# First K and a third of the first Q by the plain queue, cast in parts; the mask row table as 24 rows twice onto zeros

## The chip, the cores and the metric

One core of one Trainium2 chip runs the kernel. The metric is the device time of one execution, in microseconds, of the slowest core (here the only one). Executions of this kernel scatter by about 1 us and now and then more, also from chip to chip, so each ratio below sets a kernel against the kernel before in rounds on the same chip.

## The reference, cut to what matters

```python
# attention: batch 4, heads 8, sequence 768, head_dim 64, blocks of 32 rows
scores = q @ k^T / 8            # (4, 8, 768, 768)
mask   = |block_i - block_j| <= 1 or first/last block or 3 sampled blocks per block row
attn   = softmax(where(mask, scores, -1e9))
x      = (attn @ v), heads side by side         # (3072, 512)
# gated FFN: d_model 512, d_ff 1536
out    = (sigmoid(x @ w_gate) * (x @ w_val)) @ w_out    # (3072, 512)
```

All inputs are float32, `sampled_blocks` int64. The kernel computes in float16 with float32 accumulation.

## The kernel before

The kernel is a list of operations, each with a rough duration and a priority. A planner in the kernel (`Plan.run`) plays them through with assumed durations and landing times. Its outcome is a **fixed order** of instructions for each engine. On the chip the engines took their instructions in that order and waited where an operand was not there yet (1.60 us on ScalarE in the kernel before). So an operation that the planner thought would be ready early, but is not, holds up all that stands behind it on its engine.

Attention is done in 12 chunks of 256 queries (3 per batch), each for 4 pairs of heads; one pair of a chunk takes 3 score tiles, so 3 exps on ScalarE. The first chunk (`n == 0`) adds the mask as a bias inside the score product, the others multiply by a 0/1 mask on VectorE. FFN work for finished chunks is mixed in.

```python
FIRST = [("q", 0), ("k", 1), ("q", 1), ("k", 2), ...]    # casting loads of batch 0, in this order
# ... cut ...
# planner: when a load that was issued at `now` is assumed to have landed
                if o.dma:
                    first = now + (3.2 if e == "POOL" else 1.9)
                    if o.dma > 0.15:
                        first = dma_free = max(dma_free, first) + o.dma
                    o.seen = first + 0.3 + o.slack
# ... cut ...
# head: identity, first K and mask row table on the plain queue (SP), two small block tables on ACT's
    P.op("SP", 0.4, ... nc.sync.dma_start(ident16(), id_h.ap()) ..., prio=-99)
    P.op("ACT", 0.4, ... nc.scalar.dma_start(sbi(), sampled_blocks) ..., prio=-90)
    P.op("ACT", 0.4, ... nc.scalar.dma_start(mi(), mi_h.ap()) ..., prio=-89)
    P.op("SP", 0.5, ... nc.sync.dma_start(e24(), e24_h.ap()) ..., prio=-94.5)   # 128 rows, mostly zeros
    load("k", 0, 0, -95)
    P.op("ACT", 0.83, lambda t=t, c=c: nc.scalar.copy(c(), t()), reads=[t], writes=[c], prio=-67)
    for i, (nm, p) in enumerate(FIRST):
        last_in = load_half(nm, 0, p, -60 + i, ...)           # GpSimd: float32 in HBM to float16
    for p in range(NP):
        turn_pe("k", 0, p, every, -40 + 2 * p)                # transposes on TensorE
        turn_pe("q", 0, p, early, -39.5 + 2 * p)
# ... cut: block tables -> bias rows (VectorE, TensorE) ...
# loads of the next batch, plain queue, behind the third of three output-weight loads
                for nm in "kqv":
                    o = load(nm, b + 1, p, seq + p, behind=turned[:-2][-2:],
                             **(dict(after=[w_out[8]], sync="o") if b == 0 else {}))
                    o.slack = 1.5
                for nm in "kq":
                    turned.append(turn_dma(nm, b + 1, p, seq + p + CAST_LATE * b))   # cast, then DMA transpose
                cast_v(b + 1, p, seq + p + CAST_LATE * b)
```

The softmax here doesn't subtract the row's maximum and nothing guards it: scores larger than these inputs give would overflow.

## Time and profile before

| what | where it is read | value |
|---|---|---|
| time, median of 4 runs | result | 297.81 us (297.67 to 298.46) |
| TensorE busy | page, part 1 | 289.7 of 295.6 us |
| first exp starts | timeline | 9.03 us |
| second FFN weight landed, first gate matmul | issues, timeline | 25.1, 25.35 us |
| next batch's first load issued | timeline | 40.24 us |
| TensorE idle from 45 to 50 us | windows | 0.75 us |

Lines of the page of the kernel before: busy time by engine (part 1), and the chain that ended last (part 4).

```profile
PE 289.7 (98%) x3417; PEld 211.3 (72%) x3417; DVE 192.4 (65%) x448; ACT 212.5 (72%) x329; POOL 13.4 (5%) x22
...
PE 82%; DMA 13%; POOL 2%; issue 1%; SPq 0%; ACT 0%; DVE 0%; POOLq 0%
```

TensorE looks full. But "busy" spans overlap (a gate matmul is 0.27 us long in the page, and the next starts 0.11 us after it), and 13% of the chain of waits is DMA, all of it before 50 us.

The timeline of the head. Columns: start, duration, engine, line and operation, output and input, count, and in brackets the idle time just before with what ended it.

```profile
1.38 0.31 ACTq L338 DMA_DIRECT2D mi<-bb_mdet_iota  x1
...
3.78 0.22 DVE L509 TENSOR_TENSOR eqs<-mi,sbi 24x72 f32<-24x72 f32 x1 [2.52 <-DMA mi<-bb_mdet_iota]
...
4.11 0.83 ACT L451 CAST k_first<-ks 128x768 f16<-128x768 f32 x1 [1.10 <-DMA ks<-in_k_dram]
...
6.26 0.35 PE L427 MATMUL psum<-ident,q 128*64 128x128 f16 x4
...
7.76 0.53 PE L427 MATMUL psum<-ident,k 128*64 128x128 f16 x12 [0.28 <-DMA k<-in_k_dram]
...
8.38 0.28 PE L582 MATMUL psum<-bias,e 64*128 64x256 f16 x2
...
9.03 1.94 ACT L598 ACTIVATE pt<-psum 128x1024 f16<-128x1024 f32 x2 [4.10 <-PE psum L582]
```

The block table is there at 3.78 us. The transposes of the *next* pair's K (7.76, waiting for their load) stand ahead of the first scores (8.38).

ScalarE from 15 to 30 us: the exps of the first chunk run into those of the second (12 of the first chunk, then on), with short waits.

```profile
14.64 2.98 ACT L598 ACTIVATE pt<-psum 128x1024 f16<-128x1024 f32 x3 [0.69 <-PE psum L582]
17.85 5.71 ACT L598 ACTIVATE pt<-psum 128x1024 f16<-128x1024 f32 x6 [0.24 <-PE psum L582]
23.95 3.77 ACT L598 ACTIVATE pt<-psum 128x1024 f16<-128x1024 f32 x4 [0.39 <-PE psum L582]
```

Windows: stretch and its length, then busy time of PE, PEld, DVE, ACT, POOL (with counts), the granted clock, DMA share and GB/s.

```profile
5.00:10.00 5.00, 4.72 (x72) 2.93 (x71) 2.57 (x6) 0.97 (x2) 4.29 (x7) 1.00 1.25 180
10.00:15.00 5.00, 4.81 (x90) 3.28 (x85) 3.48 (x8) 4.26 (x6) 2.91 (x4) 1.00 1.31 202
...
20.00:25.00 5.00, 4.72 (x95) 3.51 (x92) 4.12 (x11) 4.61 (x6) 0.00 (x0) 1.00 1.16 209
...
45.00:50.00 5.00, 4.25 (x68) 3.22 (x67) 2.10 (x7) 3.76 (x7) 0.00 (x0) 1.00 1.08 286
```

The DMA share, a sum of the packets' times, passes 1 here (1.31 from 10 to 15 us). In windows of 2 us it stays at 1.13 or more from 4 to 38 us; from 38 to 41 us it falls to between 0.53 and 0, since the next batch's loads are issued only at 40.24. The timeline behind the last of these rows:

```profile
45.69 0.83 ACT L402 CAST q<-qs 128x768 f16<-128x768 f32 x1 [1.60 <-DMA qs<-in_q_dram]
...
47.19 0.83 ACT L393 CAST v<-vs 128x768 f16<-128x768 f32 x1 [0.38 <-DMA vs<-in_v_dram]
...
48.67 0.42 DVE L632 TENSOR_TENSOR x<-psum,rz 128x256 f16<-128x256 f32 x1
...
49.15 0.28 PE L657 MATMUL psum<-ident,x 128*128 128x128 f16 x2 [0.74 <-DVE x L632]
```

ScalarE stands 1.60 us in front of a cast whose load (next batch's Q) has not landed. Gate functions stand behind it, VectorE behind them, TensorE last. The last wait in this chain is not that one but the next: the cast of V, whose load landed at 47.16. A gate function follows at 47.92, VectorE at 48.33 and 48.67, TensorE at 49.15.

### The profile page before, as it was taken

Reading aid. Unit: us, or ns where it says so; the run is one execution under the profiler, and the core shown is the slowest. Engines: PE = TensorE matmul, PEld = TensorE weight load, DVE = VectorE, ACT = ScalarE, POOL = GpSimd, SP = SyncE. Lnnn points to the kernel's source line nnn. Section 1 sums busy time; section 2 is a strip of 40 time slices with the busy share of each in tenths; the row PEclk is TensorE's granted clock in tenths of the full one; section 3 lists DMA queues with packets and bytes.
Section 4 is the critical chain, followed back from the end, with each engine's and each line's share of the span. In section 5 each row is a group of like instructions: output and inputs, shape, how many; then the busy total and the mean of one; then the engine's idle time right before and its main releaser. Section 6 shows DMA issues by size and latency. Waiting matters only on the chain.

```text
span 295.6 us, 8119 instructions
## 1 busy us (share of the span) xinstructions
PE 289.7 (98%) x3417; PEld 211.3 (72%) x3417; DVE 192.4 (65%) x448; ACT 212.5 (72%) x329; POOL 13.4 (5%) x22
## 2 busy tenths in 40 slices
PE   8999998999999999999999999999999999999995
PEld 7676875786587587578578678667767768778673
DVE  3659995799677677577767657657657656634230
ACT  2699987889888789797588578478478478434331
POOL 8630000000000000000000000000000000000000
PEclk9999999999999999999999999999999999999999
DMA  7999969999999969940210210210120120120102
GB/s 157 199 211 210 206 171 283 311 297 271 272 244 248 228 96 308 172 115 2 62 47 0 65 47 3 55 54 2 31 77 2 27 83 3 27 82 0 38 35 72
DMA packets 50316, 35.56 MB, mean 120 GB/s; under 512 B 31080, under 2 KB 47336, under 8 KB 50280
## 3 DMA queue, kind: packets, MB, share of 16 engines
q1 hardware_dynamic: 43520, 28.16, 38.5%
q0 software_dynamic: 6688, 6.88, 14.1%
q8 instruction: 26, 0.43, 0.6%
q14 instruction: 10, 0.08, 0.1%
q10 hardware_dynamic: 72, 0.01, 0.0%
HBM read 28.55 MB, written 6.29 MB: 118 GB/s over the span
## 4 chain that ended last, share of the span: by engine, by line
PE 82%; DMA 13%; POOL 2%; issue 1%; SPq 0%; ACT 0%; DVE 0%; POOLq 0%
PE psum L683 40%; PE psum L727 21%; PE psum L582 10%; PE psum L621 10%; DMA wo<-in_moe_w_out_dram 8%; DMA q<-in_q_dram 3%; DMA vs<-in_v_dram 2%; POOL q L409 1%; POOL k L409 1%; POOL wo L481 1%; SPq L371 0%; POOL vh L409 0%; PE psum L657 0%; DVE h L709 0%; ACT tg L702 0%
## 5 line engine op out<-in xcount | busy, mean ns | idle before, releaser
L598 ACT ACTIVATE pt<-psum 128x1024 f16<-128x1024 f32 x144 | 143.9, 1025 | 38.1 <-PE psum L582 37.9
L606 DVE TENSOR_TENSOR pt<-pt,mask 128x1024 f16<-128x1024 f16 x132 | 90.4, 689 | 44.1 <-ACT pt L598 43.7
L683 PE MATMUL psum<-x,wg 128*128 128x256 f16 x576 | 86.6, 273 | 0.2 <-DVE h L709 0.2
L683 PE MATMUL psum<-x,wv 128*128 128x256 f16 x576 | 86.7, 273 | 0.0
L709 DVE SCALAR_TENSOR_TENSOR h<-tg,psum 128x256 f16<-128x256 f32 x144 | 56.8, 416 | 21.3 <-ACT tg L702 21.2
L727 PE MATMUL psum<-wo,h 128*128 128x512 f16 (+1 forms) x300 | 66.8, 371 | 0.0
L702 ACT ACTIVATE tg<-psum 128x256 f32<-128x256 f32 x144 | 55.2, 388 | 14.1 <-PE psum L683 11.3
L683 PEld LDWEIGHTS <-wg 128*128 128x128 f16 x576 | 54.7, 98 | 11.5 <-issue 4.2
L683 PEld LDWEIGHTS <-wv 128*128 128x128 f16 x576 | 53.8, 98 | 11.9 <-issue 6.1
L727 PEld LDWEIGHTS <-h 128*128 128x128 f16 x300 | 27.5, 98 | 30.6 <-issue 4.0
L582 PE MATMUL psum<-qT,kT 64*128 64x256 f16 x576 | 48.5, 272 | 0.3 <-ACT pt L598 0.3
L621 PEld LDWEIGHTS <-pt 128*128 128x128 f16 x1152 | 40.4, 97 | 4.3 <-issue 1.3
L621 PE MATMUL psum<-v,pt 128*128 128x65 f16 x1152 | 42.2, 193 | 0.0
L582 PEld LDWEIGHTS <-kT 64*128 64x128 f16 x576 | 23.4, 94 | 14.5 <-issue 11.0
L744 ACT ACTIVATE y<-psum 128x512 f32<-128x512 f32 (+1 forms) x21 | 12.1, 577 | 21.9 <-PE psum L727 20.0
L632 DVE TENSOR_TENSOR x<-psum,rz 128x256 f16<-128x256 f32 x48 | 20.4, 424 | 1.6
L629 DVE RECIPROCAL rz<-psum 128x4 f32<-128x4 f32 x48 | 8.6, 179 | 15.6 <-PE psum L621 15.1
L356 PE MATMUL psum<-zero 128*128 128x128 f16 x49 | 5.7, 296 | 1.0 <-DVE zero L335 1.0
L582 PE MATMUL psum<-bias,e 64*128 64x256 f16 x48 | 6.3, 273 | 0.0
L402 ACT CAST q<-qs 128x768 f16<-128x768 f32 x6 | 5.0, 833 | 1.8 <-DMA qs<-in_q_dram 1.8
L552 DVE TENSOR_SCALAR mask<-psum 128x512 f16<-128x512 f32 x9 | 6.1, 683 | 0.0
L356 PEld LDWEIGHTS <-zero 128*128 128x128 f16 x49 | 4.7, 138 | 1.8 <-DVE zero L335 1.0
(43 smaller groups left out, 72.4 us busy)
## 6 DMA issues: line engine op xcount, KB each, us to landing
out_dram<-y SPq DMA_DIRECT2D x23, 256.0 KB, 2.4
ks<-in_k_dram SPq DMA_DIRECT2D x13, 384.0 KB, 4.1
qs<-in_q_dram SPq DMA_DIRECT2D x12, 384.0 KB, 5.4
vs<-in_v_dram SPq DMA_DIRECT2D x12, 384.0 KB, 5.0
wg<-in_moe_w_gate_dram POOLq DMA_DIRECT2D x2, 768.0 KB, 14.2
wv<-in_moe_w_val_dram POOLq DMA_DIRECT2D x2, 768.0 KB, 17.0
wo<-in_moe_w_out_dram POOLq DMA_DIRECT2D x3, 512.0 KB, 21.8
q<-in_q_dram POOLq DMA_DIRECT2D x4, 192.0 KB, 6.2
```

What stands on the lines that cost most here:

```text
L356: "PE", dur, lambda: nc.tensor.matmul(t(), zero(), zero(), start=True, stop=True),
L582: nc.tensor.matmul(st()[:, hd, jj * CH : (jj + 1) * CH], l[r, 2 * tt + jj, :], m[r, 2 * c : 2 * c + 2, :], start=not (own and masked), sto ...
L598: lambda st=st, pt=pt: nc.scalar.activation(pt().rearrange("p h j q -> p h (j q)"), st(), AF.Exp, scale=SCALE),
L606: nc.vector.tensor_tensor(t, t, mask()[:, c, tt].unsqueeze(1).to_broadcast([128, 2, 512]), op=ALU.mult)
L621: nc.tensor.matmul(o()[:, 2 * jq + hd, 0:65], pts[j // 2]()[:, hd, j % 2, jq * 128 : jq * 128 + 128], v_[:, hd, j, 0:65], start=(j == 0), ...
L629: P.op("DVE", 0.2, lambda: nc.vector.reciprocal(rz(), o()[:, :, 64:65]), reads=[o], writes=[rz], prio=seq - 5)
L632: lambda: nc.vector.tensor_tensor(x16().rearrange("p j (h d) -> p (j h) d", d=64), o()[:, :, 0:64], rz().to_broadcast([128, 4, 64]), op=AL ...
L683: nc.tensor.matmul(t()[:, z : z + w], wt()[:, i, f * 128 : (f + 1) * 128], xT[g, i]()[:, 0:w], start=(i == 0), stop=(i == NP - 1),)
L702: lambda tg=tg, a=pair[0]: nc.scalar.activation(tg()[:, 0:w], a[0]()[:, a[1] : a[1] + w], AF.Tanh, scale=0.5),
L709: lambda tg=tg, a=pair[1], h_=h_: nc.vector.scalar_tensor_tensor(h_()[:, 0:w], tg()[:, 0:w], 1.0, a[0]()[:, a[1] : a[1] + w], op0=ALU.add, ...
L727: nc.tensor.matmul(py()[:, m], hts[g, f]()[:, tt * 128 : (tt + 1) * 128], wo()[:, f, m], start=(f == 0), stop=(f == NF - 1),)
L744: lambda py=py, y=y, m=m: nc.scalar.activation(y()[:, m], py()[:, m], AF.Copy, scale=0.5),
```

## The change

Its intent: bring the first exp forward. The first K goes first on the plain queue, a third of the first Q comes along uncast, ScalarE and VectorE cast only what the first scores need, 120 KB of zeros of the mask table are no longer loaded (a memset makes them), and the planner is given fixed landing times for these loads. Two things come along: value products of the first chunk are placed later, and the loads of the next batch are gated by the second output-weight load instead of the third.

```diff
+LAND_K, LAND_Q, E24 = 4.0, 4.7, 4.2
-    ("q", 0), ("k", 1), ("q", 1), ("k", 2), ("q", 2), ("v", 0), ("k", 3), ...
+    ("k", 1), ("q", 1), ("k", 2), ("q", 2), ("v", 0), ("q", 0), ("k", 3), ...
@@ planner
-                if o.dma:
+                if o.lands is not None:
+                    o.seen = o.lands
+                elif o.dma:
@@ head
-    P.op("SP", ... ident16 ..., prio=-99, dma=0.1)
-    P.op("ACT", ... sbi ..., prio=-90)      P.op("ACT", ... mi ..., prio=-89)
-    P.op("SP", ... e24, 128 rows ..., prio=-94.5, dma=0.5)
+    P.op("DVE", 0.3, lambda: nc.vector.memset(e24(), 0.0), writes=[e24], prio=-99)
+    P.op("ACT", ... ident16 ..., prio=-99, lands=3.0)
+    P.op("ACT", ... sbi ..., prio=-98, lands=3.4)
+    P.op("ACT", ... mi ..., prio=-97, lands=3.8)
+    for i, r in enumerate((0, 64)):
+        P.op("SP", ... e24()[r : r + NB] <- 24 rows ..., prio=(-96, -93)[i], lands=E24)
@@
-    load("k", 0, 0, -95)
-    P.op("ACT", 0.83, ... nc.scalar.copy(c(), t()) ..., prio=-67)
+    P.op("SP", ... k_in <- src["k"][0][:, 0:2] ..., prio=-95, lands=LAND_K)
+    P.op("SP", ... q_in <- src["q"][0][:, 0:2, early] ..., prio=-94, lands=LAND_Q)
+    P.op("ACT", 0.35, ... k_a <- k_in[:, :, early] ..., prio=-88)
+    P.op("ACT", 0.35, ... q_a <- q_in ..., prio=-88)
+    P.op("DVE", 0.42, ... k_b <- k_in[:, :, later] ..., prio=-67)
@@ block rows -> bias: the first product and its eviction now have priority -89 (were -69)
@@ value products
-        prio=seq + 0.1
+        prio=seq + (3.05 if n == 0 and p < 3 else 0.1)
@@ gate of the next batch's loads
-            if s == 2:   landed["o"] = ins        ...   after=[w_out[8]]
+            if s == 1:   landed["o"] = ins        ...   after=[w_out[4]]
# ... cut: the same in the helpers, split transposes, mask order ...
```

More of the change, by code (lines that the diff above doesn't have):

```diff
@@ L31 @@
 EDGES = [0, 768, 1536]
+LAND_K, LAND_Q, E24 = 4.0, 4.7, 4.2
 FIRST = [
-    ("q", 0), ("k", 1), ("q", 1), ("k", 2), ("q", 2), ("v", 0), ("k", 3), ("q", 3), ("v", 1), ("v", 2), ("v", 3),
+    ("k", 1), ("q", 1), ("k", 2), ("q", 2), ("v", 0), ("q", 0), ("k", 3), ("q", 3), ("v", 1), ("v", 2), ("v", 3),
 ]
@@ L56, with __init__ @@
 class Op:
-    def __init__(self, ways, deps, allocs, prio, mode, dma, behind):
+    def __init__(self, ways, deps, allocs, prio, mode, dma, behind, lands):
         self.ways, self.deps, self.allocs = ways, deps, allocs
-        self.prio, self.mode, self.dma, self.behind = prio, mode, dma, list(behind)
+        self.prio, self.mode, self.dma, self.behind, self.lands = prio, mode, dma, list(behind), lands
         self.eng = self.start = self.end = self.seen = None
@@ L83, in banks, with op @@
         self.rings["ps"] = [None] * n
-    def op(self, eng, dur, fn, reads=(), writes=(), after=(), prio=0, mode=None, dma=0.0, behind=(), alt=()):
+    def op(self, eng, dur, fn, reads=(), writes=(), after=(), prio=0, mode=None, dma=0.0, behind=(), alt=(), lands=None):
         deps, allocs = list(after), []
         ways = {eng: (dur, fn), **{e: (t, f) for e, t, f in alt}}
-        o = Op(ways, deps, allocs, prio, mode, dma, behind)
+        o = Op(ways, deps, allocs, prio, mode, dma, behind, lands)
         for b in reads:
@@ L269 @@
     tok = NJ * np.arange(128)[None, :] + np.arange(NJ)[:, None]
-    e24_np = np.zeros((128, NJ * 128), np.float16)
-    for r in (0, 64):
-        e24_np[r : r + NB] = tok.reshape(1, -1) // BLK == np.arange(NB)[:, None]
+    e24_np = (tok.reshape(1, -1) // BLK == np.arange(NB)[:, None]).astype(np.float16)
     e24_h = nc.inline_tensor(e24_np, name="bb_e24")
@@ L335 @@
     P.op("DVE", 0.1, lambda: nc.vector.memset(zero(), 0.0), writes=[zero], prio=-91)
-    P.op("SP", 0.4, lambda: nc.sync.dma_start(ident16(), id_h.ap()), writes=[ident16], prio=-99, dma=0.1)
-    P.op("ACT", 0.4, lambda: nc.scalar.dma_start(sbi(), sampled_blocks), writes=[sbi], prio=-90, dma=0.1)
-    P.op("ACT", 0.4, lambda: nc.scalar.dma_start(mi(), mi_h.ap()), writes=[mi], prio=-89, dma=0.1)
-    P.op(
-        "SP", 0.5, lambda: nc.sync.dma_start(e24().rearrange("b j q -> b (j q)"), e24_h.ap()),
-        writes=[e24], prio=-94.5, dma=0.5,
-    )
+    P.op("DVE", 0.3, lambda: nc.vector.memset(e24(), 0.0), writes=[e24], prio=-99)
+    P.op("ACT", 0.4, lambda: nc.scalar.dma_start(ident16(), id_h.ap()), writes=[ident16], prio=-99, dma=0.1, lands=3.0)
+    P.op("ACT", 0.6, lambda: nc.scalar.dma_start(sbi(), sampled_blocks), writes=[sbi], prio=-98, dma=0.1, lands=3.4)
+    P.op("ACT", 0.4, lambda: nc.scalar.dma_start(mi(), mi_h.ap()), writes=[mi], prio=-97, dma=0.1, lands=3.8)
+    for i, r in enumerate((0, 64)):
+        P.op(
+            "SP", 0.45,
+            lambda r=r: nc.sync.dma_start(e24()[r : r + NB].rearrange("b j q -> b (j q)"), e24_h.ap()),
+            writes=[e24], prio=(-96, -93)[i], dma=0.2, lands=E24,
+        ).deps[1:] = []
     vring = [one([128, 2, NJ, VW], f16, f"v16_{i}") for i in range(8)]
@@ L360 @@
     P.spin, P.spin_op, P.spin_until = zero, spin_op, SPIN
+    every, early, later = slice(0, NJ), slice(0, 2), slice(2, NJ)
     stage, half16, tr, v16 = {}, {}, {}, {}
@@ L405, in load_half @@
     def load_half(nm, b, p, prio, dur=0.72):
-        c = sb(f"{nm}16" if nm != "v" else "vh", [128, 2, NJ, 64], f16)
+        cut = (nm, b, p) == ("q", 0, 0)
+        js = later if cut else every
+        if cut:
+            c = one([128, 2, NJ - 2, 64], f16, "q16_late")
+        else:
+            c = sb(f"{nm}16" if nm != "v" else "vh", [128, 2, NJ, 64], f16)
         half16[nm, b, p] = stage[nm, b, p] = c
         o = P.op(
-            "POOL", dur, lambda: nc.gpsimd.dma_start(c(), src[nm][b][:, 2 * p : 2 * p + 2]),
-            writes=[c], prio=prio, dma=1.0,
+            "POOL", dur, lambda: nc.gpsimd.dma_start(c(), src[nm][b][:, 2 * p : 2 * p + 2, js]),
+            writes=[c], prio=prio, dma=0.8 if cut else 1.0,
         )
@@ L413, in load_half, with turn_pe @@
         return o
-    def turn_pe(nm, b, p, js, prio, behind=()):
+    def turn_pe(nm, b, p, js, prio, behind=(), c=None, j0=0):
         n = js.stop - js.start
-        c = half16[nm, b, p]
+        c = half16[nm, b, p] if c is None else c
         if (nm, b, p) not in tr:
@@ L427, in go @@
                     nc.tensor.transpose(
-                        g()[hd * 64 : hd * 64 + 64, j, :], c()[:, hd, js.start + j], ident16()
+                        g()[hd * 64 : hd * 64 + 64, j, :], c()[:, hd, js.start + j - j0], ident16()
                     )
         P.op("PE", 0.06 * n, go, reads=[c, ident16], writes=[g], prio=prio, mode="col", behind=behind)
-        P.op(
+        return P.op(
             "DVE", 0.1 + 0.075 * n, lambda: nc.vector.tensor_copy(t()[:, js], g()), reads=[g], writes=[t],
             prio=prio,
+            alt=[("ACT", 0.17 + 0.09 * n, lambda: nc.scalar.copy(t()[:, js], g()))] if prio < -80 else [],
         )
@@ L445, in turn_dma @@
         )
-    every, early, later = slice(0, NJ), slice(0, 2), slice(2, NJ)
-    load("k", 0, 0, -95)
-    t, c = stage["k", 0, 0], one([128, 2, NJ, 64], f16, "k16_first")
-    half16["k", 0, 0] = c
-    P.op("ACT", 0.83, lambda t=t, c=c: nc.scalar.copy(c(), t()), reads=[t], writes=[c], prio=-67)
+    k_in = one([128, 2, NJ, 64], f32, "k_in")
+    q_in = one([128, 2, 2, 64], f32, "q_in")
+    k_a, k_b = one([128, 2, 2, 64], f16, "k16_a"), one([128, 2, NJ - 2, 64], f16, "k16_b")
+    q_a = one([128, 2, 2, 64], f16, "q16_a")
+    P.op(
+        "SP", 0.5, lambda: nc.sync.dma_start(k_in(), src["k"][0][:, 0:2]), writes=[k_in], prio=-95, dma=1.0,
+        lands=LAND_K,
+    )
+    P.op(
+        "SP", 0.5, lambda: nc.sync.dma_start(q_in(), src["q"][0][:, 0:2, early]), writes=[q_in], prio=-94, dma=0.7,
+        lands=LAND_Q,
+    )
+    P.op("ACT", 0.35, lambda: nc.scalar.copy(k_a(), k_in()[:, :, early]), reads=[k_in], writes=[k_a], prio=-88)
+    P.op("ACT", 0.35, lambda: nc.scalar.copy(q_a(), q_in()), reads=[q_in], writes=[q_a], prio=-88)
+    P.op("DVE", 0.42, lambda: nc.vector.tensor_copy(k_b(), k_in()[:, :, later]), reads=[k_in], writes=[k_b], prio=-67)
     for i, (nm, p) in enumerate(FIRST):
         last_in = load_half(nm, 0, p, -60 + i, 0.82 if i == 0 else 0.72)
+    late = None
     for p in range(NP):
-        turn_pe("k", 0, p, every, -40 + 2 * p)
-        turn_pe("q", 0, p, early, -39.5 + 2 * p)
+        if p == 0:
+            turn_pe("k", 0, 0, early, -87, c=k_a)
+            turn_pe("q", 0, 0, early, -86.5, c=q_a)
+            late = turn_pe("k", 0, 0, later, -40, c=k_b, j0=2)
+        else:
+            turn_pe("k", 0, p, every, -40 + 2 * p)
+            turn_pe("q", 0, p, early, -39.5 + 2 * p)
         cast_v(0, p, -30 + p)
@@ L481, in go @@
             ins = nc.gpsimd.dma_start(wo()[:, 4 * s : 4 * s + 4], wov[:, 4 * s : 4 * s + 4])
-            if s == 2:
+            if s == 1:
                 landed["o"] = ins
@@ L514, in blocks, with expand @@
         d.tensor_tensor(eqs()[:, 1], eqs()[:, 1], eqs()[:, 2], op=ALU.max)
-        for r in (0, 64):
-            d.tensor_tensor(mb16()[:, r : r + NB], eqs()[:, 0], eqs()[:, 1], op=ALU.max)
-    P.op("DVE", 0.65, blocks, reads=[sbi, mi], writes=[mb16, eqs], prio=-70)
-    for c, j0, n in ((0, 0, 2), (1, 2, 4)):
+        d.tensor_tensor(
+            mb16().rearrange("p (a r) -> p a r", a=2)[:, :, 0:NB],
+            eqs()[:, 0].unsqueeze(1).to_broadcast([NB, 2, NB]),
+            eqs()[:, 1].unsqueeze(1).to_broadcast([NB, 2, NB]), op=ALU.max,
+        )
+    P.op("DVE", 0.5, blocks, reads=[sbi, mi], writes=[mb16, eqs], prio=-89)
+    def expand(j0, n, prio, behind=()):
         pb = psb([n, 128])
@@ L525 @@
             ),
-            reads=[mb16, e24], writes=[pb], prio=-69 + 32.5 * c, mode="full",
+            reads=[mb16, e24], writes=[pb], prio=prio, mode="full", behind=behind,
         )
@@ L532 @@
             ),
-            reads=[pb], writes=[bias], prio=-69 + 32.5 * c,
+            reads=[pb], writes=[bias], prio=prio,
         )
+    expand(0, 2, -89)
     mask_ops = {}
@@ L593, in attend @@
             )
+            if (n, p, tt) == (0, 0, 0):
+                o.deps.remove(late)
             scored.append(o)
@@ L626, in values @@
                         )
-        valued[n, p] = P.op("PE", 0.79, values, reads=[*pts, v16[b, p]], writes=[o], prio=seq + 0.1, mode="full")
+        valued[n, p] = P.op("PE", 0.79, values, reads=[*pts, v16[b, p]], writes=[o], prio=seq + (3.05 if n == 0 and p < 3 else 0.1), mode="full")
         P.op("DVE", 0.2, lambda: nc.vector.reciprocal(rz(), o()[:, :, 64:65]), reads=[o], writes=[rz], prio=seq - 5)
@@ L757 @@
             for p in range(NP):
-                turn_pe("q", 0, p, later, 9.0, [valued[0, 1]])
-            build_mask(1, 11.5, scored[:1])
+                turn_pe("q", 0, p, later, 9.0, [valued[0, 1]], j0=2 if p == 0 else 0)
+            expand(2, 4, 2, scored[1:2])
+            build_mask(1, 11.5, scored[4:5])
             build_mask(2, 14.5, [valued[0, 2]])
@@ L774 @@
                         nm, b + 1, p, seq + p, behind=turned[:-2][-2:],
-                        **(dict(after=[w_out[8]], sync="o") if b == 0 else {}),
+                        **(dict(after=[w_out[4]], sync="o") if b == 0 else {}),
                     )
```

## The prediction

> **What bounds it now.** TensorE, from about 25 us on. The busy table gives PE 289.7 us of a 295.6 us span, and in the timeline its matmul groups from 28.8 to 45 us start back to back. The idle that is left is early: 0.99 us before the first matmul, stretches below 10 us hidden by warming matmuls on zeros (39 of them up to 5.1 us), 0.3 and 0.2 us near 25 to 29 us, and 0.74 us at 49.15 us. Before 25 us no FFN matmul can run: the second FFN weight lands at 25.1 us (issued 10.9, 14.2 us to landing) and the first gate matmul starts at 25.35. In that head ScalarE paces: the first exp starts at 9.03 us, one takes about 0.98 us back to back, and from 10 to 25 us it is busy 13.6 of 15 us.
>
> **What the first exp waits for (timeline).** K issued 1.15, landed 4.05; cast of all 768 columns 0.83 us; transposes 5.26; Q transposes only after them, 6.26; first mask bias copies from 6.87; the transposes of the next K stand ahead of the scores and wait for their load until 7.76; scores 8.38, exp 9.03. The 192 KB mask table lands only at 5.9, Q at 6.03.
>
> **What changes.** K is issued first on its queue (about 0.74, so landing near 3.7); 120 KB of table zeros no longer travel; a third of Q (128 KB) comes uncast on the same queue. [...] in 3 to 6 us the table took 1.85 us after K. Scaling that, I estimate the Q third at 4.9 to 5.2. Then a cast of 256 columns (0.35, estimated from 0.83 for 768), 4 transposes 0.35, copy 0.29, hand-overs about 0.2 each: scores near 6.5, first exp at 7.1 (6.7 to 7.6), 1.9 us earlier. The next K no longer stands ahead of them. Added: a 0.3 us memset, extra small copies, all on idle engines.
>
> Cast loads land 0.97 us apart; K1, Q1, K2, Q2 move forward one place, so exps should run without the 0.69 and 0.24 us gaps at 14 and 17.6 us. When the FFN starts, attention is ahead by 2.2 to 2.7 exps.
>
> **Worth on the critical path.** Not 1.9 us in full: one exp carries about 0.5 us of PE work (scores 0.27, a third of a value product of 0.77), so 1.1 to 1.4 us of PE work is pulled into the head. FFN weights land perhaps 0.3 us earlier. Next-batch loads now follow the second output-weight load (about 37.5 us, not 40.2), sharing with the third. ScalarE waited 1.60 us for a Q of that batch at 45.69, and that led to the 0.74 us PE gap; most of it should go. Sum: about 2.1 us.
>
> **Predicted: 295.8 us, range 294.2 to 297.2.** Faster by over 2%: 0.03; within 2%: 0.95; slower: 0.02.
>
> **Signs.** Right: first exp near 7.1; twelfth exp ending near 19.5 instead of 21.7; first gate matmul still near 25; next-batch loads issued near 37.5; gap at 49 gone; PE busy total falls little, span by 2. Wrong: the Q third landing past 5.8, exps stalling on Q3 or V, or gate matmuls waiting.
>
> **What would make it wrong.** The fixed order was planned with assumed landings; if a load is late, an engine blocks in order and the gain is lost. The third output-weight load, slowed by sharing, may hold the first output matmul. If the head work is limited by loads rather than exps, only some 0.7 us remains; if all the shift survives, 3 us.

The sum came to about 2.1 us (1.1 to 1.4 of work pulled forward, 0.3 for the weights, most of the 0.74 us gap), 297.87 less 2.1 makes 295.8. The landing of the Q third rests on the 1.85 us of the mask table alone. The hand-overs of about 0.2 us were the author's estimate; in the trace of the kernel before, TensorE starts 0.32 us after the cast of K ends and VectorE 0.05 us after the transposes. For the 0.3 us of the weights no source is given. Nor was it shown that sharing slows the third output weight: it landed 23.9 us after its issue in the changed kernel, 23.3 before.

## The result, and the profile after

The changed kernel takes 299.80 us (median of 4 runs, 298.99 to 300.04) against 297.81. The ratio is 1.0058, with a 95% interval from 1.0034 to 1.0082: slower by 0.6%, where a gain of 0.7% was predicted. A ratio here is the mean time of one kernel's fast runs over that of the other's of the same rounds, so it is not quite the ratio of the medians that are quoted. Executions over 1.5% slower than the fastest of the same kernel are left out of the means.

The page of the changed kernel:

```profile
PE 289.8 (97%) x3407; PEld 210.9 (71%) x3407; DVE 191.7 (64%) x447; ACT 213.1 (71%) x333; POOL 13.4 (4%) x22
...
PE 82%; DMA 13%; POOL 2%; ACT 1%; SPq 1%; issue 1%; POOLq 0%
```

TensorE's busy total is the same and the span is 2.7 us longer: time was added in which TensorE had nothing to do, or did it at half rate. The head in the timeline:

```profile
1.89 0.30 ACTq L340 DMA_DIRECT2D mi<-bb_mdet_iota  x1
...
4.29 0.41 ACT L470 CAST k_a<-k_in 128x256 f16<-128x256 f32 x1 [0.78 <-DMA k_in<-in_k_dram]
...
6.16 0.22 DVE L536 TENSOR_TENSOR eqs<-mi,sbi 24x72 f32<-24x72 f32 x1 [4.51 <-DMA mi<-bb_mdet_iota]
...
6.97 0.28 PE L553 MATMUL psum<-e,mb 24*128 24x256 f16 x1 [2.02 <-DVE mb L542]
...
7.08 0.41 ACT L471 CAST q_a<-q_in 128x256 f16<-128x256 f32 x1 [2.38 <-DMA q_in<-in_q_dram]
...
8.10 0.85 PE L437 MATMUL psum<-ident,k 128*64 128x128 f16 x12
...
9.21 0.42 PE L437 MATMUL psum<-ident,q 128*64 128x128 f16 x4
...
9.56 0.40 PE L613 MATMUL psum<-bias,e 64*128 64x256 f16 x2
...
10.64 3.77 ACT L631 ACTIVATE pt<-psum 128x1024 f16<-128x1024 f32 x4 [1.92 <-PE psum L613]
```

The first exp is at 10.64 us, 1.6 us later than before and 3.5 us later than predicted. K is there at 4.29, but the block table only at 6.16 (before: 3.78) and the Q third at 7.08 (predicted: 4.9 to 5.2). The product of the block table stands first on TensorE, so the ready K waits behind it. TensorE idles 2.02 us, and the next pair's K and Q (8.10, 9.21) again stand ahead of the scores. Compare durations: these 12 transposes took 0.53 us before and 0.85 now, two bias matmuls 0.28 and 0.40. TensorE is running at half rate here: the windows view gives a granted clock of 0.50 from 8 to 11 us.

ScalarE from 15 to 30 us:

```profile
14.28 4.78 ACT L631 ACTIVATE pt<-psum 128x1024 f16<-128x1024 f32 x5
19.39 2.85 ACT L631 ACTIVATE pt<-psum 128x1024 f16<-128x1024 f32 x3 [0.32 <-PE psum L613]
24.29 3.77 ACT L631 ACTIVATE pt<-psum 128x1024 f16<-128x1024 f32 x4 [2.05 <-PE psum L613]
```

The exps of the first chunk do run without the old waits, but there is a new hole of 2.05 us after the twelfth. TensorE has the remaining Q transposes (20.36 to 21.9 us) and two whole value products (21.94 to 23.6) in its order ahead of the second chunk's scores. The windows:

```profile
5.00:10.00 5.00, 3.03 (x42) 2.04 (x44) 2.72 (x9) 1.15 (x3) 4.02 (x6) 0.78 1.23 180
10.00:15.00 5.00, 5.00 (x74) 2.97 (x71) 1.15 (x4) 4.36 (x5) 3.92 (x6) 0.87 1.33 201
...
20.00:25.00 5.00, 4.82 (x102) 3.59 (x98) 3.86 (x12) 2.95 (x4) 0.00 (x0) 1.00 1.16 210
...
45.00:50.00 5.00, 3.60 (x48) 2.86 (x47) 3.38 (x8) 3.96 (x7) 0.00 (x0) 1.00 1.21 248
```

The granted clock falls to 0.78 and 0.87. And the idle time of TensorE between 45 and 50 us, of which the prediction expected most to go, has grown from 0.75 to 1.40 us:

```profile
45.84 0.83 ACT L398 CAST v<-vs 128x768 f16<-128x768 f32 x1 [1.91 <-DMA vs<-in_v_dram]
...
46.99 0.42 DVE L742 SCALAR_TENSOR_TENSOR h<-tg,psum 128x256 f16<-128x256 f32 x1 [1.15 <-ACT tg L735]
...
47.47 0.92 PE L654 MATMUL psum<-v,pt 128*128 128x65 f16 x24 [0.38 <-DVE h L742]
...
47.88 0.56 DVE L405 CAST q<-qs 128x768 f16<-128x768 f32 x1 [0.47 <-DMA qs<-in_q_dram]
...
49.09 0.27 PE L575 MATMUL psum<-bias,e 64*128 64x256 f16 x1 [0.70 <-DVE mask L583]
...
50.02 1.89 PE L760 MATMUL psum<-wo,h 128*128 128x512 f16 x8 [0.34 <-DVE h L742]
```

The pattern is that of before: a cast in ScalarE's order waits for a load, now V, and the rest waits behind it. The largest single piece, 0.70 us at 49.09, stands behind a mask on VectorE that comes after another such cast, of Q (47.88).

### An account of TensorE's work

To say where the 2.7 us of these two executions went, count the matmuls of each kind in a stretch and weight them with the spacing that the traces show while TensorE is full: gate matmuls 0.44 us per 4, output 2.6 us per 12, scores 0.54 us per 8, value products 0.77 us per 24; the bias and mask products of 256 columns are given the weight of a score. Transposes are left out. This is an estimate from counts, not a measured time.

| stretch | before | after | difference |
|---|---|---|---|
| to 25 us | 11.4 | 10.4 | -1.0 |
| 25 to 45 us | 17.7 | 17.0 | -0.7 |
| 45 to 60 us | 13.7 | 12.4 | -1.3 |
| 60 to 100 us | 38.9 | 38.8 | about 0 |

By 60 us the changed kernel is 3.0 us of work behind, and its span is 2.7 us longer. From there both run alike. This held in every usable trace: span plus work done by 60 us is 337.8 to 338.9 us in all of them (from the table below; matmuls at the edge of a stretch can be counted either way, which moves an entry by up to 0.4 us). So the whole case lies in the first 60 us, in two parts: the head, and the stretch around 48 us.

### The profile page after: what moved, and what is told of

It reads as the page before. It is cut to its first block, busy times and chain, and to the rows that moved or that the text cites. A ratio compares the mean times of both kernels' runs of the same rounds, so it can differ in the third digit from the quotient of the medians.

```text
span 298.3 us, 8111 instructions
## 1 busy us (share of the span) xinstructions
PE 289.8 (97%) x3407; PEld 210.9 (71%) x3407; DVE 191.7 (64%) x447; ACT 213.1 (71%) x333; POOL 13.4 (4%) x22
## 4 chain that ended last, share of the span: by engine, by line
PE 82%; DMA 13%; POOL 2%; ACT 1%; SPq 1%; issue 1%; POOLq 0%
PE psum L716 40%; PE psum L760 21%; PE psum L613 10%; PE psum L654 10%; DMA wo<-in_moe_w_out_dram 7%; DMA vs<-in_v_dram 3%; DMA vh<-in_v_dram 3%; SPq L376 1%; POOL k L419 1%; POOL q L419 1%; ACT pt L631 1%; POOL q_late L419 0%; POOL vh L419 0%; PE psum L690 0%; ACT y L777 0%
## 5 line engine op out<-in xcount | busy, mean ns | idle before, releaser
L735 ACT ACTIVATE tg<-psum 128x256 f32<-128x256 f32 x144 | 55.1, 388 | 15.3 <-PE psum L716 12.4
L716 PEld LDWEIGHTS <-wg 128*128 128x128 f16 x576 | 54.5, 98 | 10.7 <-issue 3.6
L716 PEld LDWEIGHTS <-wv 128*128 128x128 f16 x576 | 53.8, 98 | 11.5 <-issue 5.7
L613 PEld LDWEIGHTS <-kT 64*128 64x128 f16 x576 | 23.4, 95 | 15.1 <-issue 11.7
L662 DVE RECIPROCAL rz<-psum 128x4 f32<-128x4 f32 x48 | 8.5, 178 | 16.5 <-PE psum L654 16.0
L407 ACT CAST k<-ks 128x768 f16<-128x768 f32 x8 | 6.7, 833 | 1.2 <-DMA ks<-in_k_dram 1.2
L398 ACT CAST v<-vs 128x768 f16<-128x768 f32 x7 | 5.8, 832 | 2.1 <-DMA vs<-in_v_dram 2.1
L360 PE MATMUL psum<-zero 128*128 128x128 f16 x39 | 4.4, 290 | 1.4 <-DVE zero L336 1.4
## 6 DMA issues: line engine op xcount, KB each, us to landing
wg<-in_moe_w_gate_dram POOLq DMA_DIRECT2D x2, 768.0 KB, 13.8
```

What stands on the lines that cost most here:

```text
L407: alt=[("ACT", 0.83, lambda: nc.scalar.copy(c(), s().rearrange("p h j d -> p j h d")))],
L613: nc.tensor.matmul(st()[:, hd, jj * CH : (jj + 1) * CH], l[r, 2 * tt + jj, :], m[r, 2 * c : 2 * c + 2, :], start=not (own and masked), sto ...
L662: P.op("DVE", 0.2, lambda: nc.vector.reciprocal(rz(), o()[:, :, 64:65]), reads=[o], writes=[rz], prio=seq - 5)
L716: nc.tensor.matmul(t()[:, z : z + w], wt()[:, i, f * 128 : (f + 1) * 128], xT[g, i]()[:, 0:w], start=(i == 0), stop=(i == NP - 1),)
L735: lambda tg=tg, a=pair[0]: nc.scalar.activation(tg()[:, 0:w], a[0]()[:, a[1] : a[1] + w], AF.Tanh, scale=0.5),
```

## The experiments

Theories at the start: **A**, the late block table sets the start; **B**, the late Q third does; **C**, the earlier gate of the next loads costs the time. Later came **D**: what a head gains or loses is partly given back at 45 to 52 us. There a cast of the next batch stands too early in a fixed order, while its load lands at a time that the head does not move. Its rival **E**: TensorE has simply run out of first-batch work there.

All results in one table. "First exp", work and gaps are from one profiled execution each; ratios are to the kernel before, in the rounds of that call. Medians of different calls come from different chips, so compare ratios.

| run | ratio (95%) | median us | first exp us | work by 25 / 25-45 / 45-60 | PE idle 45-50, 50-55 us | span us |
|---|---|---|---|---|---|---|
| before | 1 | 297.81 | 9.03 | 11.4 / 17.7 / 13.7 | 0.75, 0 | 295.6 |
| after | 1.0058 (1.0034-1.0082) | 299.80 | 10.64 | 10.4 / 17.0 / 12.4 | 1.40, 0.11 | 298.3 |
| tables_first | 1.0084 (1.0052-1.0115) | 300.30 | 11.00 | 9.6 / 16.9 / 13.8 | 0, 0 | 297.9 |
| tables_q_first | 1.0038 (1.0002-1.0074) | 299.00 | 9.42 | 11.2 / 17.2 / 12.4 | 1.67, 0 | 297.4 |
| hold_casts | 1.0186 (1.0147-1.0224) | 303.09 | 11.46 | 8.0 / 15.5 / 13.7 | 0, 0 | 301.7 |
| gate_undone | 1.0038 (1.0008-1.0068) | 298.78 | 10.48 | 10.0 / 17.1 / 14.1 | 0, 0 | 296.9 |
| gate_alone | 1.0030 (1.0003-1.0056) | 298.44 | 10.34 | 10.8 / 17.3 / 14.4 | 0, 0 | 296.3 |
| tq_gate | 1.0044 (0.9998-1.0090) | 299.17 | 8.51 | 11.5 / 17.9 / 10.2 | 2.55, 0 | 298.6 |
| told | 1.0002 (0.9976-1.0028) | 297.38 | 8.12 | 11.6 / 17.6 / 13.2 | 0.96, 0.50 | 296.0 |
| told_turn | 1.0024 (1.0006-1.0042) | 298.20 | 8.19 | 12.2 / 17.3 / 12.5 | 0.46, 1.32 | 296.3 |
| after_late | 0.9997 (0.9957-1.0038) | 298.28 | 11.73 | 10.0 / 17.0 / 14.0 | 0, 0 | 297.0 |
| told_late | 0.9993 (0.9952-1.0034) | 297.71 | 8.26 | 11.7 / 17.5 / 14.6 | 0, 0 | 294.6 |
| told_turn_late | 0.9949 (0.9900-0.9998) | 296.48 | - | - | - | - |
| before_late | 0.9957 (0.9909-1.0004) | 296.18 | 9.70 | 11.4 / 17.3 / 14.5 | 0, 0 | 294.6 |
| after_warm | 1.0084 (1.0046-1.0122) | 300.46 | 10.08 | 10.9 / 17.3 / 10.7 | 2.20, 0 | 299.7 |
| delay_before | 1.0046 (1.0006-1.0085) | 299.67 | 11.76 | 9.4 / 16.5 / 14.4 | 0, 0 | 298.5 |
| delay_late | 1.0030 (0.9994-1.0067) | 298.86 | 12.22 | 9.4 / 16.7 / 14.2 | 0, 0 | 297.6 |
| told_turn_late2 | 0.9967 (0.9924-1.0010) | 297.23 | 8.45 | 12.0 / 17.4 / 14.4 | 0, 0 | 294.1 |

All kernels gave correct results. Of the twelve kernels not named "late", the six whose first exp came by 10.1 us all idle at 45 to 55 us (0.75 to 2.55 us); of the six with a later first exp only the changed kernel does. How long they idle does not follow the first exp (0.75 us at 9.03, 2.20 us at 10.08). The traced runs named "late" have none whatever their head. Each of these idle times is from one execution.

One profile of a head is not the head. In three traces the instructions of the old head run in the same order, and the first exp comes at 9.03, 9.70 and 10.34 us (before, before_late, gate_alone). The changed head gives 10.48, 10.64 and 11.73 (gate_undone, after, after_late), with the Q third landing at 6.77, 7.05 and 7.82. So the change did make the first exp later, but a difference under about 1 us between two single profiles shows little.

### tables_first

```diff
-    P.op("ACT", ... ident16 ..., prio=-99, lands=3.0)      # issued before sbi and mi
+    P.op("ACT", ... ident16 ..., prio=-96, lands=3.0)      # issued after them
```

> The changed kernel with one edit: on ScalarE's queue the two small block tables are issued before the identity instead of after it; the order of all instructions on the other engines is kept. In the changed kernel the block table landed at 6.1 us and the Q third at 7.08; the first exp began at 10.64 instead of 9.03. Theory A (the block table, which stands first in VectorE's and TensorE's order, sets the start): it lands near 3.8 again, the first exp begins near 8 and the time falls by 1.5 us or more. Theory B (the Q third sets the start): mask product and K transposes move forward, but the scores still wait for Q at about 7; first exp 9.5 to 10.3, time falls by less than 0.7 us.

The block table was there at 4.34 us (5.60 to 7.04 in the four traces that issue it behind the identity beside the casting loads), so its lateness came mainly from standing behind the identity on ScalarE's queue. The first exp did not improve (11.00), since Q came at 7.79 in this run, as theory B has it. The range of B was missed on the late side, and a new wait shows what I had not thought of: the identity is now last on that queue and late itself.

```profile
4.34 0.22 DVE L536 TENSOR_TENSOR eqs<-mi,sbi 24x72 f32<-24x72 f32 x1 [2.68 <-DMA mi<-bb_mdet_iota]
...
7.03 0.30 PE L437 MATMUL psum<-ident,k_a 128*64 128x128 f16 x4 [1.60 <-DMA ident<-bb_ident]
```

### tables_q_first

```diff
  (as tables_first)
-    q_in: prio=-94        k_in: prio=-95
+    q_in: prio=-97        k_in: prio=-96.5                 # Q third first, then K
```

> As tables_first, and the Q third is also issued before K on the plain queue. Both theories together: Q lands near 3.5, K near 5, the block table near 3.8; first exp between 6.5 and 7.5; the time about 2.5 to 4 us below the changed kernel (296 to 297), at or below the kernel before. If the start is not what costs the time (theory C: the later gate of the next loads costs it), the first exp moves but the time stays above 299.

The block table came at 3.99 and the Q third at 2.96, 2.2 us after its issue; K, now second in the queue, came at 5.41 (4.29 in the changed kernel). The first exp came at 9.42, not at 7. Timeline of tables_q_first:

```profile
5.72 0.40 ACT L471 CAST q_a<-q_in 128x256 f16<-128x256 f32 x1
...
8.53 0.30 PE L437 MATMUL psum<-ident,q 128*64 128x128 f16 x4 [0.79 <-DMA q<-in_q_dram]
...
9.42 2.85 ACT L631 ACTIVATE pt<-psum 128x1024 f16<-128x1024 f32 x3 [1.82 <-PE psum L613]
```

The first scores were ready to run, but in TensorE's order they stand behind the next pair's Q, whose casting load lands at 8.5. So a third cause lies in the order itself. And with a first exp 0.4 us later than in the kernel before, the time was still 1.1 us longer (1.0038): TensorE idled 1.67 us at 45 to 50 us.

### hold_casts

```diff
+    first casting load: manual dependency on the landing of k_in
```

> The changed kernel, but GpSimd's first casting load waits until K has landed, so that the early plain loads have the DMA engines to themselves; plain queues untouched. If contention with the casting loads made them late: block table landed by 4.2 us, Q third by 5.0, first exp 7 to 8. If they are late by themselves[...]: block table still near 6, Q near 7, first exp still 10.6. The time is no verdict here, since all casting loads and the FFN weights come 2 to 3 us later; expected 1 to 2 us slower than the changed kernel.

Without casting loads beside them, the Q third landed 3.5 us after its issue (5.3 in the changed kernel) and the block table was there at 5.21 (6.16). Timeline of hold_casts:

```profile
5.21 0.22 DVE L545 TENSOR_TENSOR eqs<-mi,sbi 24x72 f32<-24x72 f32 x1 [3.55 <-DMA mi<-bb_mdet_iota]
5.33 0.40 ACT L480 CAST q_a<-q_in 128x256 f16<-128x256 f32 x1 [0.45 <-DMA q_in<-in_q_dram]
```

So sharing with the casting loads cost the Q third about 1.8 us; in the four traces with this head beside them it took 5.0 to 6.1 us. For the block table, which was expected by 4.2, less is shown: beside the casting loads this head had it at 5.60 to 7.04, so 5.21 is only just outside the scatter, and its place in the queue (tables_first) counts for more. The first exp did not come at 7 to 8 but at 11.46, because the next pair's loads, which stand ahead of the scores, were held too, and two bias matmuls again took 0.42 us from 10.8 us on (0.28 in the kernel before). The time, 303.09, was to be slower by design; it missed the expected 1 to 2 us above the changed kernel by more than 1 us.

### gate_undone, gate_alone, tq_gate: theory C

```diff
 gate_undone (on the changed kernel) and tq_gate (on tables_q_first):
-    if s == 1: ...   after=[w_out[4]]
+    if s == 2: ...   after=[w_out[8]]
 gate_alone (on the kernel before): the opposite edit
```

> The changed kernel with the loads of the next batch gated by the third output-weight load again, as in the kernel before, instead of the second. Theory C (the earlier loads, sharing the engines with the third output weight, cause the larger TensorE gap at 45 to 50 us): the gap of 1.4 us there shrinks and the time falls by 0.5 to 1.5 us, to 298.3 to 299.3. Rival (the gap comes from the late start and the fixed order): time unchanged within 0.4 us or slower.

> The kernel before with one part of the change alone: the loads of the next batch wait for the second output-weight load instead of the third. If this part costs about 1 us wherever it stands (as gate_undone suggests, 299.8 to 298.8): 298.3 to 299.0, with a TensorE gap near 45 to 50 us larger than the 0.75 us of before. If it only hurts together with the late start: 297.4 to 298.1. If it helps, as I predicted: below 297.2.

> tables_q_first (tables first, Q third first, K next) with the gate of the next loads as in the kernel before. If the two costs add: 299.0 minus 1.0, so 297.7 to 298.3, first exp near 9.4 as in tables_q_first, no TensorE gap at 45 to 50 us. If they do not add, 298.6 or more.

gate_undone fitted theory C: no gap, and 1.0 us less by the medians; by the ratios, 1.0038 against 1.0058, it is 0.6 us, which is not clear of the noise. (Its head was slow too: two bias matmuls took 0.40 us at 9.4 us, 0.28 in the kernel before. The windows view prints a clock of 1.00 there, but the clock record of this trace begins only at 13.29 us; where nothing is recorded, 1.00 is printed, as in the kernel before from 4 to 6 us, where the record begins at 6.40.) gate_alone was 0.9 us slower than before, but not by a gap: its trace has none. The head of that execution was late by itself (K could be cast at 5.18 us instead of 4.11, then a clock of 0.50 from 8 to 11 us, first exp 10.34), with a head whose code is unchanged; how much of the 0.9 us is the gate stays open. tq_gate refuted theory C: with the old gate and the earliest head so far (first exp 8.51), the profiled execution had the *largest* gap, 2.55 us, then a clock of 0.69 from 50 to 55 us. Its four times are 300.37, 300.47, 297.95 and 297.98, with granted clocks of 0.994, 0.994, 1.000 and 0.999: the long gap and the slow clock behind it seem to have struck two executions of four. I read from this that the gap is a matter of how far the head runs ahead of the loads, and that the gate is only one of the things that shift it; that the earlier gate costs time is not shown.

### told and told_turn: the planner told what the runs showed

```diff
 told = tq_gate and
-LAND_K, LAND_Q, E24 = 4.0, 4.7, 4.2        ident16 lands=3.0
+LAND_K, LAND_Q, E24 = 4.6, 3.2, 4.8        ident16 lands=4.6
                 if o.lands is not None:
                     o.seen = o.lands
+                    if o.dma > 0.15:
+                        dma_free = max(dma_free, now + 1.9) + o.dma
 told_turn = told and
-                turn_pe("q", 0, p, later, 9.0, [valued[0, 1]], ...)
+                turn_pe("q", 0, p, later, 11.0, [scored[9]], ...)
```

> tq_gate, and the kernel's own planner is told the landings that the runs showed: identity, K, Q third and mask table at their measured times, and the plain loads counted as taking the engines ahead of the casting loads. The planner then puts the next pair's Q transposes behind the first scores. First exp 8.2 to 8.8 instead of 9.4. If an earlier first exp is worth half of itself: 0.3 to 0.6 us below tq_gate. If the time is set elsewhere (the FFN weights at 25 us and the order after the twelfth exp): within 0.2 us of tq_gate.

> told, with the remaining Q transposes of the first batch released earlier (after the tenth score tile, not the second value product) and placed lower, so that scores of the second chunk come before the last value products. In the changed kernel ScalarE idles 2.05 us between the twelfth and the thirteenth exp; here that hole should be under 0.8 us. If the hole is what ate the gain: 0.5 to 1.0 us below told, to about 296.5 to 297.2, faster than the kernel before. If not: within 0.3 us of told.

told brought the first exp to 8.12 and the time to that of the kernel before (1.0002); that is 1.8 us below tq_gate by the medians, more than expected, though tq_gate had two runs with the long gap. told_turn did close the hole after the twelfth exp (0.6 us more work by 25 us than told). It was not faster but 0.8 us slower by the medians (1.0024 against 1.0002, so not clear of the noise): in its trace the gap at 45 to 55 us took the gain back (work from 45 to 60 us 12.5 instead of 13.2). What engines waited for in told between 40 and 55 us (total, times, longest):

```profile
DVE v L398 <- DMA vs<-in_v_dram: 2.8, 1, 2.8
ACT q L409 <- DMA qs<-in_q_dram: 2.6, 2, 2.2
```

### after_late, told_late, told_turn_late, before_late: theory D against E

```diff
-                    o.slack = 1.5       # planner's allowance for the landing of the next batch's loads
+                    o.slack = 4.5
```

> The changed kernel with one number: the planner assumes that the loads of the next batch land 3 us later than it did (slack 4.5 us instead of 1.5), so that VectorE's and ScalarE's fixed orders put the casts of these loads later; the loads are issued as in the changed kernel. Theory D (the gain of an early head is lost between 45 and 52 us, because a cast standing in a fixed order waits for a load whose landing the head does not move, and masks, gates and TensorE wait behind it): waits for those loads fall from 2.1 us to under 0.7, the TensorE gap at 45 to 50 us from 1.4 to under 0.5 us, time 0.7 to 1.3 us below the changed kernel (298.5 to 299.1). Rival E (TensorE has simply run out of work of the first batch there): gap and time unchanged within 0.3 us.

> told with the same number. In told VectorE waited 2.8 us for V and ScalarE 2.6 us for Q of the next batch and TensorE had gaps of 0.96 and 0.5 us between 45 and 55 us. Theory D: gaps together under 0.5 us, time 0.7 to 1.3 us below told, 296.1 to 296.7, ratio to before about 0.995 to 0.998. Rival E: unchanged, 297.2 to 297.6.

> told_turn with the same number: the head without the hole behind the twelfth exp. Theory D and the hole both count: below told_late by 0.3 us or more, 295.6 to 296.3. If the hole costs nothing: equal to told_late within 0.2 us. Rival E: like told_turn, 298.2.

> The kernel before with the same number, as a control. Its gap at 45 to 50 us was 0.75 us in one profile. Theory D: gap gone, up to 0.7 us faster, 297.0 to 297.5. It also says what the rest of the change is worth when this loss is gone from both sides: told_late minus before_late should be near minus 0.8 us if an early first exp is worth half of itself, 0 if nothing.

In all three traces of these four (told_turn_late has no usable one) the waits for those loads are gone from the list of longest waits, and TensorE has no idle time in the windows from 45 to 55 us. The rows 45 to 50 us of told_late and of before_late:

```profile
45.00:50.00 5.00, 5.00 (x68) 3.12 (x67) 3.83 (x9) 4.36 (x6) 0.00 (x0) 1.00 0.79 242
```

```profile
45.00:50.00 5.00, 5.00 (x81) 3.62 (x78) 4.62 (x13) 4.89 (x7) 0.00 (x0) 1.00 1.26 268
```

There was work to do, so E falls and D stands for the gap. The loads are issued under the same conditions, but more than the place of the casts has changed: the DMA transposes that follow them were issued 3.2 to 3.9 us later (44.19 to 47.50 us for the first in before and before_late). In after_late the first V landed 6.0 us after its issue instead of 6.6, in told_late 5.3 instead of 6.8. This rival, that the transposes slow the loads, was not tested by itself. In before_late V landed later than in before (7.1 instead of 6.0 us) and yet nothing waited for it, so there the place of the casts is enough.

The times agree for the changed kernel (1.0058 to 0.9997) and for the kernel before (0.9957), with intervals of 0.4 to 0.5% either way; the second still includes 1. told_late did not become faster by its median (297.71; told 297.38, on another chip), although its profiled execution ran 1.4 us shorter than told's. The chip of this call scattered more: its eleven runs of the kernel before lie between 296.73 and 300.26. The profile of told_turn_late fell on the execution at half rate (0.22 us from start to start); its other five times are 295.31 to 298.95.

With the gap gone on both sides, after_late is still 0.4% above before_late by the ratios (0.7% by the medians, 298.28 and 296.18). This is what the rest of the change may cost, its head included, but the intervals overlap and do not exclude nothing. told_late against before_late was to show what an early head is worth: about 0.8 us was expected if half of it counts. It came out 0.4% slower by the ratios, within the noise, and the two profiled spans are the same (294.6) with first exps at 8.26 and 9.70. So no gain of an early head is shown.

### after_warm, delay_before, delay_late: what a head is worth

```diff
 after_warm (on the changed kernel): each warming matmul twice
+    ... for _ in range(2 if dur > 0.1 else 1)
 delay_before (on before), delay_late (on before_late):
-    lambda t=t, c=c: nc.scalar.copy(c(), t())
+    lambda t=t, c=c: [nc.scalar.copy(c(), t()) for _ in range(3)]     # same result, 1.66 us later
```

> The changed kernel with twice as many warming matmuls on zeros before the first real work (about 70 instead of 35, so TensorE is busy up to about 7 us instead of 4.9); the order of everything else is kept. In the changed kernel TensorE idled 2.0 us before the mask product, and transposes and the first scores then ran at half rate until about 11 us. If the slow clock delayed the first exp: transposes and scores at the full rate, first exp 0.7 to 1.0 us earlier (9.6 to 10.0). The worth of that in time, at half a microsecond per exp and with the gap at 45 to 50 us unchanged or larger: 0 to 0.4 us below the changed kernel.

> The kernel before with the cast of the first K made three times (same result), so that its head starts 1.66 us later; nothing else touched. First exp 10.3 to 10.9 instead of 9.0. Theory D (what a head gains or loses before 25 us is given back at 45 to 50 us, where a cast waits for a load that the head does not move): attention is behind by 1 to 2 exps at 25 us, the gap of 0.75 us at 45 to 50 us goes, time 0 to 0.4 us above before. If a late head costs its own length: plus 1.3 to 1.7 us.

> before_late (no gap at 45 to 50 us) with the same delay of the head. Here nothing is left to give back: 0.5 to 1.0 us above before_late, so a ratio to before of about 0.997 to 0.9995 where before_late had 0.9957. If the head is worth nothing even here: 0.9957 again.

after_warm kept the rate up: transposes 0.50 and bias matmuls 0.28 us instead of 0.85 and 0.40. The first exp came 0.56 us earlier, although the longer warming itself held TensorE until the first product at 7.41 (6.97 in the changed kernel; the block table was there at 5.81). From that product to the first exp it took 2.67 us instead of 3.67. 0.5 us more work was done by 25 us. The time rose to 300.46, which by the ratios (1.0084 against 1.0058) is not clear of the noise. Windows of after_warm:

```profile
45.00:50.00 5.00, 2.80 (x45) 2.43 (x43) 2.73 (x8) 3.34 (x7) 0.00 (x0) 1.00 1.27 214
50.00:55.00 5.00, 5.00 (x40) 2.37 (x40) 3.36 (x9) 3.43 (x4) 0.00 (x0) 0.66 1.12 350
```

A mended head in the changed kernel made the gap at 45 to 50 us larger (2.20 us instead of 1.40), and after it the clock was 0.66 from 50 to 55 us. In this execution the head's gain was more than taken back. Three of its six executions have a granted clock of 0.993 or 0.994 and took 300.93 to 301.51 us, the other three 299.47 to 299.99.

delay_before was a miss: I had expected next to nothing. With the delay came a slow clock too (0.50 from 10 to 15 us), and the first exp came 2.7 us later, not 1.7, and the time rose by 1.4 us by the ratio (0.2 to 2.5; 2.1 by the medians of its rounds). The gap did go, as theory D says, but that gives back only the 0.75 us that it held. delay_late against before_late: first exp 2.5 us later, 2.7 us by the medians (0.7% by the ratios, on two chips, with 0.6% either way). So without the gap this late head cost about its own length, twice the half that I had reckoned with. Part of it may be the slow rate, though: in delay_late two bias matmuls took 0.40 to 0.42 us at 11 to 13 us (0.28 at 14.1 us; the windows view prints a clock of 1.00 for both). A late head at full rate was not tried.

### told_turn_late2

The same file as told_turn_late.

> The same kernel as told_turn_late, whose profile fell on an execution[...] (571 us), so that it has no usable trace, and one of its six times was a further 3 us above the rest. Ratio to before 0.992 to 0.996 (295.5 to 296.7 us); in the trace first exp near 8.3, more TensorE work done by 25 us than any other kernel, no gap at 45 to 52 us.

First exp 8.45, no gap, work by 25 us near the most of any kernel (12.0; told_turn 12.2), and the shortest profiled span, 294.1 us. The ratio, 0.9967, lies just above the expected range and its interval includes 1. Of the two looks at this kernel one interval excludes 1 and one does not. It is likely about 1 us faster than the kernel before. Against before_late, which is one number away from the kernel before, no gain can be told.

## Why the prediction was wrong, point by point

1. **"The Q third at 4.9 to 5.2 ... first exp at 7.1."** This is the step that failed first. The Q third came at 7.08 and the first exp at 10.64. I scaled a landing from the mask table's bytes, but the Q third stands behind K in its queue and shares the engines with the casting loads. Shown by hold_casts (3.5 instead of 5.3 us to landing) and by tables_q_first (2.2 us when it is issued first). Of the 3.5 us by which the first exp missed, about 2.0 is this landing. Another 0.84 is point 3, and the rest, about 0.7, is the chain of casts, transposes and scores, which was slower than reckoned, in part for the clock (point 4).
2. **The identity's move was not costed at all.** It went ahead of the small tables on ScalarE's queue. The block table came at 6.16 instead of 3.78, and it is first in the new order of VectorE and TensorE. tables_first brought it to 4.34: behind the 32 KB identity the 4.5 KB table was in use 4.27 us after its issue, ahead of it 2.92 us. By itself it did not set the first exp, since the Q third came later still; it left TensorE idle for 2.02 us.
3. **"The next K no longer stands ahead of them."** Wrong. The next pair's K and Q still precede the first scores on TensorE. In the changed kernel the scores' own operands were ready at 8.72 us and the scores began at 9.56. In tables_q_first this alone held the scores until 8.77. I read the change of priorities and not the order that comes of it.
4. **The slow clock** was missing. After 2.02 us without work TensorE ran at half rate (granted clock 0.50) from 7.84 to 11.25 us. after_warm, without the idle stretch, ran at the full rate (two bias matmuls 0.28 us instead of 0.40) and needed 1.0 us less from the first product to the first exp. The length of the idle stretch alone does not settle it: half rate followed 1.14 us in gate_alone (two bias matmuls 0.40 us) and not 1.11 us in told_turn_late2 (0.28 us).
5. **"When the FFN starts, attention is ahead by 2.2 to 2.7 exps."** The old waits did go, as predicted. But the reordered value products and Q transposes made a hole of 2.05 us after the twelfth exp. At 25 us attention was behind by 2 tiles (56 score matmuls instead of 64). told_turn showed that the hole can be closed and is worth 0.6 us of work by 25 us.
6. **"That led to the 0.74 us PE gap; most of it should go."** The waiting engine was named rightly; the load was not (V's landing at 47.16 ended the last wait before that gap), and the cure was wrong. The loads were issued at 37.98 us, as predicted (about 37.5). But the planner moved the casts forward with them, and the gap grew to 1.40 us. The second V was 8.4 us on its way; that the third output weight slowed it is not shown, since with the old gate it took 8.6 us in tq_gate and 8.4 in told. The "late" runs show what cures it: casts, and the transposes behind them, placed later. TensorE's idle time from 45 to 55 us went from 0.75 (before), 1.51 (the changed kernel) and 1.46 us (told) to nothing.
7. **"One exp carries about 0.5 us of PE work", so half of the shift counts.** For a late head this was too low: delay_late cost about its own length, slow rate included. For an early head in a kernel with the gap it was too high: in their traces told_turn and after_warm gained work early and gave it back at 47 to 52 us.

What the 2 us consist of: by the account of work, 1.7 us of head (until 45 us) and 1.3 us more around 50 us, in the profiled pair. By the ratios, what is left without the gap is 0.4% (after_late against before_late) of the 0.6%, but the intervals are too wide to be sure of this split. Not tried alone were the 24-row table, the memset, the later value products of the first chunk and the new order of the masks; nothing in the traces points at the first two. The worth of the gate by itself is open, since gate_alone ran with a late head. What bounded the kernel was half right: TensorE sets the time from 60 us on (busy all of the 230 us from 60 to 290 in both traces). Until then it is the landings (the three largest entries of the chain of waits up to 60 us in the kernel before are loads, 63% together), and the fixed orders built on guesses of them.

## What to carry to other kernels

In a kernel with fixed orders, moving a load means asking three things: what stands ahead of it in its own queue (the block table came at 6.16 us behind the identity, 4.34 ahead of it), what shares the engines at that moment (the Q third took 5.3 us beside the casting loads, 3.5 without), and which instruction that was ready will now stand behind it (the first scores of the changed kernel were ready at 8.72 us and began at 9.56). Check the assumed landings against the trace before judging any gain; one cast placed too early stopped VectorE for 2.8 us in told, and the engine that shows the idle time can be the third in line. Work pulled forward is only kept if the next landing that is waited for moves forward too: count the work done by several points in time in both traces, and look for the stretch in which the lead is lost.
